# Weight conversion on a float64-fed attention and softplus kernel: fewer instructions per weight block, a planner that knows a shared port, and padded tiles

## The chip, the cores and the metric

The kernel runs on one core of a Trainium2 chip. The metric is the device time of one execution in microseconds (us). A profiled execution also has a span, from its first to its last instruction. Engines are named as in the profile: PE (TensorE matmul), PEld (its weight loads), DVE (VectorE), ACT (ScalarE), POOL (GpSimd) and SP (SyncE, which here only issues DMAs).

## The reference, cut to what matters

Attention with random features, for 8 batches, 8 heads, 576 tokens and head width 64, and then two dense layers with a softplus between them, for all 4608 tokens:

```
def phi(x):                                   # x: q or k, scaled
    proj = einsum('bhsd,md->bhsm', x, omega)  # 128 features
    h = proj - sum(x * x, -1) / 2
    return exp(h - max(h, -1)) / sqrt(m)
kv  = einsum('bhsm,bhsd->bhmd', phi(k), v);  z = sum(phi(k), axis=2)
x   = einsum('bhsm,bhmd->bhsd', phi(q), kv) / (einsum('bhsm,bhm->bhs', phi(q), z) + 1e-6)
h   = x.reshape(4608, 512) @ w_in             # 512 x 2048
g   = maximum(h, 0) + log1p(exp(-abs(h)))
out = (g @ w_out).astype(float32)             # 2048 x 512
```

`w_in` and `w_out` arrive as float64, 8 MB each. The chip computes in 32 bits, so the kernel turns each weight's two 32-bit words into a float32 first.

## The kernel before, in words

**Work and order.** Nothing loops on the chip. The kernel describes every piece of work as a `Work` with the engines that may do it and a cost on each, a due time, the works it comes after, and the buffers it takes and gives back. `in_order` then runs through them once, always starts what can start first, within a patience per engine chooses what is due first, and for work with a choice takes the engine whose clock plus cost plus a `LEAN` comes out least. `AHEAD` says how far beyond the earliest open due time it may look. The order in which it starts works is the order in which instructions are emitted, and each engine runs its instructions in that order. The due times are a table of numbers written into the calls (`due + 0.41` and so on). `with_fill` puts small idle matmuls (`fill`) into planned holes of PE in the first 70 us of the plan.

**Attention.** A quad is half a batch (4 heads); 16 of them. Each has units of 128 tokens per head pair: `plan_unit` loads q or k (`load`), squares it (`squares`, on POOL or ACT) and sums the squares (`norms`, DVE), projects with `omf` (`project`, PE), takes the row maximum (`maxima`, DVE), forms the bias in two tiny DVE instructions (`less_norms`, `bias`) and exponentiates (`exponent`, ACT). For k, `outer` accumulates k-features times v on PE. For q, `den` (DVE), `invert` (DVE), `divide` (POOL or DVE), `turn` (PE transposes) and `turned` follow, and `plan_x` makes x and splits it into two parts of reduced precision, `xh` and `xl`. The first two quads are early: they run before any dense layer can.

**Dense layers.** Tokens go in 3 blocks of 256 and 10 of 384, each in 16 steps (one per 128 columns of `w_in`), 208 steps in all. `plan_step`: `layer1` is 12 matmuls into `h`; then `magnitude`, `decay`, `log` (three ACT instructions), `plus` (DVE), `high` (DVE or ACT, writes `gh`), `low` (DVE or POOL, writes `gl`), and `layer2`, three matmuls of 512 columns for each 128 tokens.

**Weights.** There are 32 blocks of weights, 16 of `w_in` (names with `i`) and 16 of `w_out` (`o`). A step needs one of each. `plan_weights` loads a block of 512 KB as pairs of words, `low` and `high`, and converts it in 512-element instructions: `low_bits` scales the low word so that its three highest bits remain as an integer (L231 on ACT, L233 on DVE); `rebias` multiplies the high word, read as a float32, by 2^-112, which turns the float64 exponent into a float32 one (L239 ACT, L241 DVE); `high_bits` shifts it left by 3 into a tile of its own, `wt` (L245, DVE); `sign` puts the sign bit back (L249, DVE); `both` adds the low bits (L253, DVE or POOL); `high_part` rounds to the reduced precision of the matmul (L257, ACT or DVE); `low_part` keeps the rest (L260, DVE or POOL). That is seven instructions a block, 224 in all.

**Pools.** Tiles are placed one behind the other in pools. `halves`, two floats wide, is the last small tile before the loads, the weights and everything that follows.

## Time and profile before

| | |
|---|---|
| median of 3 runs | 1140.86 us (1138.83 to 1142.14) |
| the profiled execution | 1142.8 us, its span 1140.9 us |
| instructions in the profile | 19083 |
| busy, of the span | PE 1103.1 us, DVE 618.1, ACT 665.0, POOL 415.7 |
| mean granted clock of PE | 0.969 |

Busy time is a sum over the whole span, which has two very different parts: until about 175 us the weights come in, are converted, and PE has holes; after that PE has hardly any. So the profile is read by stretches of time. In the lists of groups, each row names the source line, engine, operation, what is written and read with its shape, the count, the busy time and the mean of one, and after the last bar the idle time of the engine before these instructions with what ended it. Durations of neighbouring instructions of one engine overlap a little in the records.

### The profile page before, as it was taken

What the parts mean: (1) busy time and instruction counts of PE and PEld (TensorE: products, weight loads), DVE (VectorE), ACT (ScalarE), POOL (GpSimd) and SP (SyncE); (2) the same over time, 40 slices, a digit from 0 to 9 for tenths busy, and PEclk for the clock granted to TensorE, in tenths of its full rate; (3) what the DMA queues carried; (4) which work ended last, traced back from release to release, by engine and by line L of the source; (5) the groups of instructions that cost most, each with busy time, mean ns of one, the idle gap of its engine ahead of it and who ended that gap; (6) DMA issues with size and microseconds to landing.
All of it is one profiled execution on the core that took longest, in us unless ns stands there. A gap on an engine that the chain in (4) does not pass through costs nothing.

```text
span 1140.9 us, 19083 instructions
## 1 busy us (share of the span) xinstructions
PE 1103.1 (97%) x6662; PEld 954.0 (84%) x6662; DVE 618.1 (54%) x1884; ACT 665.0 (58%) x1700; POOL 415.7 (36%) x428
## 2 busy tenths in 40 slices
PE   9887879999999999999999999999999999999998
PEld 8864768888888888888888888888888888899997
DVE  6979996777566264654364474554365356111111
ACT  4766646666666465565565565665565556455544
POOL 3638774434333233323242333333233333222222
PEclk6878889999999999999999999999999999999999
DMA  9722122331312031211222030211223020000000
GB/s 344 272 85 97 61 69 76 85 108 46 90 61 75 10 117 29 77 68 38 69 69 76 10 117 29 88 48 44 55 65 98 1 77 17 1 28 1 28 1 28
DMA packets 35088, 78.70 MB, mean 69 GB/s; under 512 B 5680, under 2 KB 12464, under 8 KB 34992
## 3 DMA queue, kind: packets, MB, share of 16 engines
q1 hardware_dynamic: 34992, 77.48, 21.2%
q8 instruction: 53, 0.87, 0.3%
q14 instruction: 43, 0.35, 0.1%
HBM read 67.99 MB, written 9.47 MB: 68 GB/s over the span
## 4 chain that ended last, share of the span: by engine, by line
PE 84%; DVE 2%; ACT 0%; issue 0%; POOL 0%; DVEq 0%
PE h L612 12%; PE acc L641 12%; PE acc L643 11%; PE acc L642 11%; PE h L614 11%; PE h L613 11%; PE kv L434 4%; PE ppq L349 3%; PE xp L568 3%; PE ppk L349 3%; PE tpq L521 2%; PE kv L429 1%; DVE smk L375 0%; DVE junk L505 0%; DVE wto L249 0%
## 5 line engine op out<-in xcount | busy, mean ns | idle before, releaser
L635 POOL TENSOR_TENSOR gl<-u,gh 128x384 fp32r<-128x384 f32 (+1 forms) x207 | 201.8, 976 | 581.8 <-ACT gh L631 507.3
L612 PE MATMUL h<-xh,wi 128*128 128x384 f32 (+1 forms) x832 | 282.7, 340 | 13.6 <-DVE u L627 11.6
L627 DVE SCALAR_TENSOR_TENSOR u<-h,u 128x384 f32<-128x384 f32 (+1 forms) x208 | 108.3, 521 | 337.7 <-ACT u L624 323.5
L614 PE MATMUL h<-xh,wi 128*128 128x384 f32 (+1 forms) x832 | 271.7, 327 | 0.0
L613 PE MATMUL h<-xl,wi 128*128 128x384 f32 (+1 forms) x832 | 271.4, 326 | 0.0
L641 PE MATMUL acc<-wo,gh 128*128 128x512 f32 x576 | 236.7, 411 | 0.3 <-ACT qq L533 0.3
L643 PE MATMUL acc<-wo,gl 128*128 128x512 f32 x576 | 228.7, 397 | 0.0
L642 PE MATMUL acc<-wo,gh 128*128 128x512 f32 x576 | 227.8, 396 | 0.0
L618 ACT ACTIVATE u<-h 128x384 f32<-128x384 f32 (+1 forms) x208 | 97.9, 471 | 218.3 <-PE h L614 212.4
L612 PEld LDWEIGHTS h<-xh,wi 128*128 128x128 f32 x832 | 158.1, 190 | 36.1 <-DVE u L627 14.9
L613 PEld LDWEIGHTS h<-xl,wi 128*128 128x128 f32 x832 | 158.5, 191 | 6.4
L614 PEld LDWEIGHTS h<-xh,wi 128*128 128x128 f32 x832 | 158.3, 190 | 0.0
L505 DVE CUSTOM_DVE_ANT_0 junk<-phq,zb 128x128 f32<-128x128 f32 x280 | 127.7, 499 | 15.7 <-ACT phq L382 14.7
L643 PEld LDWEIGHTS acc<-wo,gl 128*128 128x128 f32 x576 | 108.9, 189 | 26.0
L641 PEld LDWEIGHTS acc<-wo,gh 128*128 128x128 f32 x576 | 109.4, 190 | 24.3 <-issue 5.5
L631 ACT CAST gh<-u 128x384 fp32r<-128x384 f32 (+1 forms) x193 | 95.7, 496 | 54.7 <-PE acc L642 39.2
L642 PEld LDWEIGHTS acc<-wo,gh 128*128 128x128 f32 x576 | 109.9, 191 | 14.8
L382 ACT ACTIVATE phk<-ppk,smk 128x128 f32<-128x128 f32 x252 | 74.1, 376 | 61.5 <-DVE smk L375 59.6
L621 ACT ACTIVATE u<-u 128x384 f32<-128x384 f32 (+1 forms) x208 | 106.0, 510 | 4.3
L624 ACT ACTIVATE u<-u 128x384 f32<-128x384 f32 (+1 forms) x208 | 105.1, 505 | 4.6
L382 ACT ACTIVATE phq<-ppq,smq 128x128 f32<-128x128 f32 x252 | 73.3, 378 | 47.7 <-DVE smq L375 46.2
L514 POOL TENSOR_TENSOR phq<-phq,dnq 128x512 f32<-128x512 f32 (+1 forms) x70 | 67.2, 971 | 51.0 <-DVE dnq L510 48.8
(91 smaller groups left out, 1306.7 us busy)
## 6 DMA issues: line engine op xcount, KB each, us to landing
xk<-kx SPq DMA_DIRECT2D x28, 512.0 KB, 3.6
xq<-qx SPq DMA_DIRECT2D x28, 512.0 KB, 4.3
out<-o SPq DMA_DIRECT2D x36, 256.0 KB, 2.2
rawi<-wi SPq DMA_DIRECT2D x16, 512.0 KB, 6.1
rawo<-wo SPq DMA_DIRECT2D x16, 512.0 KB, 4.5
vk<-vv SPq DMA_DIRECT2D x28, 260.0 KB, 3.9
xk<-k SPq DMA_DIRECT2D x10, 386.0 KB, 6.8
zb<-zd SPq DMA_DIRECT2D x14, 256.0 KB, 4.4
```

The source lines that it names most:

```text
L382: nc.scalar.activation(b["ph"][:, c], b["pp"][j][:, t], AF.Exp, bias=b["sm"][:, 2, c : c + 1])
L505: nc.vector.tensor_tensor_reduce(jk[r, c], ph[r, c], q.zb[r, h], 1.0, 1e-6, ALU.mult, ALU.add, dn[r, 0, c : c + 1])
L612: nc.tensor.matmul(b["h"], wh, xh[:, cc, t], start=cc == 0, stop=False)
L613: nc.tensor.matmul(b["h"], wh, xl[:, cc, t], start=False, stop=False)
L614: nc.tensor.matmul(b["h"], wl, xh[:, cc, t], start=False, stop=cc == NCC - 1)
L621: nc.scalar.activation(b["u"], b["u"], AF.Exp, scale=-1.0)
L624: nc.scalar.activation(b["u"], b["u"], AF.Ln, bias=1.0)
L627: nc.vector.scalar_tensor_tensor(b["u"], b["h"], 0.0, b["u"], ALU.max, ALU.add)
L635: (nc.vector if e == "DVE" else nc.gpsimd).tensor_tensor(b["gl"], b["u"], b["gh"].bitcast(F32), ALU.subtract)
L641: nc.tensor.matmul(acc[tt], gh, w2[fc][:, 0], start=fc == 0, stop=False)
L642: nc.tensor.matmul(acc[tt], gh, w2[fc][:, 1], start=False, stop=False)
L643: nc.tensor.matmul(acc[tt], gl, w2[fc][:, 0], start=False, stop=fc == NFC - 1)
```

## The change

The conversion of a weight block becomes five instructions:

```
-        def rebias(e):
...
-                nc.scalar.activation(h, h, AF.Copy, scale=2.0**-112)
...
-        def high_bits():
...
-            nc.vector.tensor_scalar(box["f"], box["high"], 3, None, ALU.logical_shift_left)
-        def sign():
...
-        def both(e):
...
+        def rebias():
             h = box["high"].bitcast(F32)
+            nc.scalar.activation(h, h, AF.Prelu, scale=2.0**-112, alpha=2.0**32)
+        def joined():
+            h = box["high"]
+            nc.vector.scalar_tensor_tensor(h, h, 3, box["low"], ALU.logical_shift_left, ALU.bitwise_or)
```

The leaky ReLU (`Prelu`) multiplies negative values by a further 2^32. That raises the exponent field by 32, and the shift by 3 moves this bit to the place of the sign, while the old sign falls off. So one DVE instruction, `joined` (L253 after), shifts and ORs in the low bits, in place. For the OR, the low bits must stay in three bits: `low_bits` scales by 0.936 x 2^-29 on ACT (L241 after) or takes a minimum with 7 on DVE (L243 after). `rebias` (L249 after) is on ACT alone. `high_part` (L257) and `low_part` (L260) read the raw tile in place of `wt`, which is gone with its buffers; `NT2`, the number of those and of output tiles, goes from 3 to 2.

The planner treats DVE works that are marked `port=True`, and all POOL works, as users of one thing that only one of them can hold:

```
+    port = [0.0]
+    def ready(w, e, data):
+        return max(clock[e], data, port[0] if e == "POOL" or e == "DVE" and w.port else 0.0)
...
+        if e == "POOL" or e == "DVE" and w.port:
+            port[0] = w.end
```

Marked are the weight works on DVE, `less_norms`, `bias`, `den`, `divide`, `high` and `low`. `with_fill` also compares places in the order, not times alone, before it lends a bank. The first bank of a unit is given back after its first `exponent` as before, but that of an early query only after its second.

The planner's numbers change throughout, for instance:

```
-AHEAD = 33.61                                  +AHEAD = 43.01
-MARGIN = 0.34                                  +MARGIN = 0.00
-LEAN = {"DVE": 0.69, "POOL": -0.7, "ACT": 0.17}
+LEAN = {"DVE": 0.75, "POOL": 0.50, "ACT": 0.19}
-SPREAD = ((0, 25), (18, 63.28))                +SPREAD = ((0, 23.46), (18, 70.83))
-        l = do(("DVE", "POOL"), (dve(n), pool(n)), due - 0.48 + .2, low, ...)
+        l = do(("DVE", "POOL"), (dve(n), pool(n)), due - 1.63 + .2, low, ..., port=True)
```

`MARGIN` is what PE is planned to start after its data. Small tiles are padded, so that everything lies on multiples of 64 bytes: `halves` from 2 to 16 floats, `sm` from 3 to 4 rows of 8, `dn` from 2 to 4 rows of 4, `z` from 4 to 16, `v` to 528.

What the built programs show: POOL's rows fall from 433 to 97. Of its 207 `low` works 23 stay, of 80 `divide` 41, of 91 `squares` 14, of 26 `low_part` 8, and its 18 `both` are gone. DVE takes 185 `low` (1 before), 39 `divide` (0), 24 `low_part` (6), 12 `turned` (0); ACT takes 90 `squares` (13), 32 `rebias` (27), 32 `high_part` (26), 24 `low_bits` (26). PE's matmuls are the same but for the fills.

On DVE, in the part where steps and conversions run side by side, this stood before around the sixth step (`wti` and `wto` are the tiles that go away, `rawi` and `rawo` the loaded words):

```order
285 L245 TENSOR_SCALAR wto_1139<-rawo_671 128x512
286 L253 ISA wti_1107<-rawi_647,wti_1107 128x1024
287 L249 SCALAR_TENSOR_TENSOR wto_1139<-rawo_671,wto_1139 128x512
288 L245 TENSOR_SCALAR wti_1162<-rawi_709 128x512
289 L245 TENSOR_SCALAR wto_1167<-rawo_749 128x512
290 L249 SCALAR_TENSOR_TENSOR wti_1162<-rawi_709,wti_1162 128x512
291 L249 SCALAR_TENSOR_TENSOR wto_1167<-rawo_749,wto_1167 128x512
292 L375 SCALAR_TENSOR_TENSOR smk_0_0_1058<-smk_0_0_1058 128x4
```

and this stands there now (L635 is `low`, L627 `plus`, L260 `low_part`, L253 `joined`, L362 `maxima`):

```order
277 L635 TENSOR_TENSOR gl_4_1133<-u_4_1046,gh_4_1125 128x256
278 L253 SCALAR_TENSOR_TENSOR rawi_625<-rawi_625 128x512
279 L253 SCALAR_TENSOR_TENSOR rawo_661<-rawo_661 128x512
280 L362 TENSOR_REDUCE smk_0_0_841<-ppk_0_0_0_1114 128x4
281 L627 SCALAR_TENSOR_TENSOR u_5_1130<-h_5_1083,u_5_1130 128x256
282 L260 TENSOR_TENSOR wi_1159<-rawi_625,wi_1159 128x512
283 L253 SCALAR_TENSOR_TENSOR rawi_677<-rawi_677 128x512
284 L260 TENSOR_TENSOR wo_1168<-rawo_661,wo_1168 128x512
```

Two or three instructions for a block became one in place, and `low` and `low_part` have moved in beside it. On POOL, in the middle of the wide steps, one `low` per step stood before, with `divide` (L514) and `squares` (L333) between:

```order
197 L635 TENSOR_TENSOR gl_1_4541<-u_1_4429,gh_1_4518 128x384
198 L333 TENSOR_TENSOR xk_0_0_4544<-xk_0_0_4544 128x512
199 L635 TENSOR_TENSOR gl_2_4600<-u_2_4488,gh_2_4592 128x384
200 L635 TENSOR_TENSOR gl_3_4654<-u_3_4568,gh_3_4651 128x384
201 L514 TENSOR_TENSOR phq_0_4_4621<-phq_0_4_4621,dnq_0_4_0_4636 128x256
```

Now POOL has this there, one `low` in a dozen steps or so:

```order
58 L635 TENSOR_TENSOR gl_2_4439<-u_2_4354,gh_2_4429 128x384
59 L514 TENSOR_TENSOR phq_0_2_4433<-phq_0_2_4433,dnq_0_2_1_4493 128x512
60 L514 TENSOR_TENSOR phq_0_4_4613<-phq_0_4_4613,dnq_0_4_0_4630 128x256
61 L635 TENSOR_TENSOR gl_15_5138<-u_15_5070,gh_15_5135 128x384
62 L514 TENSOR_TENSOR phq_1_4_5268<-phq_1_4_5268,dnq_1_4_0_5289 128x256
```

and DVE, in the same wide steps, has `low` between its own work:

```order
1236 L635 TENSOR_TENSOR gl_3_6276<-u_3_6167,gh_3_6264 128x384
1237 L337 TENSOR_REDUCE smk_0_4_6279<-xk_0_4_6234 128x2
1238 L627 SCALAR_TENSOR_TENSOR u_4_6242<-h_4_6195,u_4_6242 128x384
1239 L577 TENSOR_TENSOR xl<-xp_1_0_0_6282,xh 128x256
1240 L577 TENSOR_TENSOR xl<-xp_1_0_1_6285,xh 128x256
1241 L627 SCALAR_TENSOR_TENSOR u_5_6309<-h_5_6289,u_5_6309 128x384
1242 L635 TENSOR_TENSOR gl_4_6329<-u_4_6242,gh_4_6327 128x384
```

So what POOL did behind DVE's back, DVE now does in its own queue, behind whatever stands there.

More of the change, by code (lines that the diff above doesn't have):

```diff
@@ L38 @@
 FILL = 0.3
[L39 to L41 removed]
+PATIENCE = {"PE": 0, "DVE": 0.02, "ACT": 0, "POOL": 0.00, "SP": 0.55}
+LEAN = {"DVE": 0.75, "POOL": 0.50, "ACT": 0.19}
+SPREAD = ((0, 23.46), (18, 70.83))
 VW = 512 + 4 * (D + 1)
@@ L55, with __init__ @@
 class Work:
-    def __init__(self, on, due, emit, after=(), take=(), give=(), delay=0.15, spare=0, behind=None):
-        self.on, self.due, self.emit = on, due, emit
+    def __init__(self, on, due, emit, after=(), take=(), give=(), delay=0.15, spare=0, behind=None, port=False):
+        self.on, self.due, self.emit, self.port = on, due, emit, port
         self.after = [w for w in after if w is not None]
@@ L128, in with_fill @@
     last, all_ = None, []
-    for w in out:
+    for i, w in enumerate(out):
         if w.engine == "PE":
@@ L132, in with_fill @@
             n = int((t - last - FILL) / 0.2135) if last is not None and t < until else 0
-            names = [b for b in banks if all(x1 <= last or x0 >= t for x0, x1 in held.get(b, []))] if n > 0 else []
+            names = [
+                b for b in banks if all(x1 <= last and g < i or x0 >= t and f >= i for x0, x1, f, g in held.get(b, []))
+            ] if n > 0 else []
             if names:
@@ L176, in favor_softplus_kernel @@
     nc.vector.tensor_scalar(omf, f, float(D) ** -0.25, None, ALU.mult)
-    halves = const.tile([P, 2], F32, name="halves")
+    halves = const.tile([P, 16], F32, name="halves")[:, :2]
     nc.vector.memset(halves, 0.0)
@@ L268, in plan_weights @@
         aw, dw, dw2, pw = act(DM), dve(DM), dve(DM, 2), pool(DM)
-        a = do(("ACT", "DVE"), (aw, dw2), due, low_bits, after=[l])
-        b = do(("ACT", "DVE"), (aw, dw2), due, rebias, after=[l])
-        c = do(
-            "DVE", dw2, due, high_bits, after=[b] + (in_w if last else []), take=[("wt", box, "t"), ("w", box, "w")],
+        a = do(("ACT", "DVE"), (aw, dw2), due, low_bits, after=[l], port=True)
+        b = do("ACT", aw, due, rebias, after=[l])
+        c = do("DVE", dw, due, joined, after=[a, b], port=True)
+        d = do(
+            ("ACT", "DVE"), (aw, dw), due, high_part, after=[c] + (in_w if last else []), take=[("w", box, "w")], port=True,
         )
         if not last:
-            in_w.append(c)
-        c = do("DVE", dw, due, sign, after=[c])
-        d = do(("DVE", "POOL"), (dw, pw), due, both, after=[a, c], give=[(box, "raw")])
-        e = do(("ACT", "DVE"), (aw, dw2), due, high_part, after=[d])
-        return do(("DVE", "POOL"), (dw, pw), due, low_part, after=[e], give=[(box, "t")])
+            in_w.append(d)
+        return do(("DVE", "POOL"), (dw, pw), due, low_part, after=[d], give=[(box, "raw")], port=True)
     class Quad:
@@ L385, in plan_unit @@
         ld = do(
-            "SP", dma(size), due - 5.26, load, behind=prev.get("load"),
+            "SP", dma(size), due - 5.46, load, behind=prev.get("load"),
             take=[("w" if early else "x", b, "x")], delay=DL, spare=2 if early else 0,
@@ L394, in plan_unit @@
         if not cols:
-            r = do("DVE", dve(w), due + 0.2, norms, after=[s], behind=prev.get("norms"), take=sm)
+            r = do("DVE", dve(w), due - 0.39, norms, after=[s], behind=prev.get("norms"), take=sm)
             prev["norms"] = r
@@ L536, in plan_queries @@
         d = do(
-            "DVE", 1.7 * f, due + 0.45 + .1, den, after=es + [q.zc], take=[("dn", b, "dns")],
-            give=[(q.slots, "zb")] if u == NU - 1 else [],
-        )
-        d = do("DVE", 0.09, due + 0.72, invert, after=[d])
-        v = do(("POOL", "DVE"), (1.0 * f, dve(n * M)), due + 0.45 + .2, divide, after=[d], give=[(b, "dns")])
+            "DVE", 1.7 * f, due + 1.01 + .1, den, after=es + [q.zc], take=[("dn", b, "dns")],
+            give=[(q.slots, "zb")] if u == NU - 1 else [], port=True,
+        )
+        d = do("DVE", 0.09, due + 0.48, invert, after=[d])
+        v = do(("POOL", "DVE"), (1.0 * f, dve(n * M)), due - 0.45 + .2, divide, after=[d], give=[(b, "dns")], port=True)
         t = do(
-            "PE", 0.108 * n, due - 0.16, turn, after=[v], behind=prev.get("turn"), give=[(bu, "phs" if q.b else "x")] if last else [],
+            "PE", 0.108 * n, due + 0.61, turn, after=[v], behind=prev.get("turn"), give=[(bu, "phs" if q.b else "x")] if last else [],
             take=[(any_, b, "tpb")] + ([("q", qt, "tag")] if u in (0, 2) else []),
@@ L547, in plan_queries @@
         h = do(
-            ("ACT", "DVE"), (act(n * M, PSUM), dve(n * M)), due + 1.1, turned, after=[t], give=[(b, "tpb")],
+            ("ACT", "DVE"), (act(n * M, PSUM), dve(n * M)), due + 0.97, turned, after=[t], give=[(b, "tpb")],
         )
@@ L680, in store @@
                 nc.sync.dma_start(out[t0 + tt * P : t0 + (tt + 1) * P, :], o["t"])
-            a = do("DVE", 0.34, due - 2.18, left, after=[ends[tt]], take=[("t2", o, "s")])
-            r = do("ACT", 0.27, due - 2.18, right, after=[a], give=[(box, ("acc", i, tt))])
-            do("SP", 0.75, due + 3.6, store, after=[a, r], give=[(o, "s")], delay=2.0)
+            a = do("DVE", 0.34, due + 1.48, left, after=[ends[tt]], take=[("t2", o, "s")])
+            r = do("ACT", 0.27, due - 0.39, right, after=[a], give=[(box, ("acc", i, tt))])
+            do("SP", 0.75, due + 8.51, store, after=[a, r], give=[(o, "s")], delay=2.0)
     assert NQ == 2
```

108 lines of the change are left out of this document (50 added, 58 removed).

## The prediction

> **What bounds the kernel now.** I read stretches of time first, since shares of the whole span mix two different parts. The columns are the stretch, its length, busy time (and count) of each engine, PE's granted clock, DMA share and rate.
>
> ```profile
> span 1140.9 us, 19083 instructions
> core 0: us, PE busy (x) PEld busy (x) DVE busy (x) ACT busy (x) POOL busy (x), PEclk, DMA share, GB/s
> 0.00:40.00 40.00, 37.42 (x214) 33.85 (x214) 28.38 (x105) 19.93 (x57) 18.42 (x28) 0.66 0.97 364
> 40.00:75.00 35.00, 26.44 (x186) 21.78 (x184) 29.84 (x104) 25.11 (x59) 18.17 (x14) 0.85 0.45 155
> 75.00:175.00 100.00, 78.77 (x465) 65.38 (x464) 96.04 (x190) 62.91 (x166) 68.88 (x54) 0.85 0.22 69
> 175.00:300.00 125.00, 124.52 (x930) 106.41 (x928) 86.78 (x300) 82.13 (x251) 49.62 (x62) 1.00 0.29 84
> 300.00:1100.00 800.00, 799.07 (x4698) 694.25 (x4697) 371.37 (x1177) 457.53 (x1134) 251.47 (x262) 1.00 0.16 51
> 1100.00:1141.00 41.00, 36.91 (x180) 32.35 (x178) 5.73 (x11) 17.37 (x35) 9.12 (x9) 0.98 0.05 20
> ```
>
> From 175 us on PE is full at full clock: of 925 us until 1100 it idles 1.4. The change leaves its matmuls alone, so nothing can be won there, only lost. What can be won lies before 175. The first 40 us belong to the transfers (0.97 of the DMA engines). From 75 to 175 us DVE is busy 96.0 of 100 us, while PE runs 465 matmuls in a time in which 175 to 300 runs twice as many at full clock. The list of PE's waits for 75 to 175 agrees, and so does one for 0 to 75 (line waited at, what ended it: us in total, times, longest):
>
> ```profile
> PE h L612 <- DVE u L627: 11.6, 7, 3.4
> PE xp L568 <- DVE smq L375: 4.9, 2, 4.6
> ```
>
> Why DVE is full is seen in the order of time, DVE first, then POOL (start, duration):
>
> ```profile
> 99.98 0.41 DVE L245 TENSOR_SCALAR wti<-rawi 128x512 uint32<-128x512 uint32 x1
> 105.80 0.68 DVE L249 SCALAR_TENSOR_TENSOR wto<-rawo,wto 128x512 uint32<-128x512 uint32 x1
> 106.74 1.52 DVE L245 TENSOR_SCALAR wto<-rawo 128x512 uint32<-128x512 uint32 x1
> 109.33 1.78 DVE L249 SCALAR_TENSOR_TENSOR wto<-rawo,wto 128x512 uint32<-128x512 uint32 x1
> ...
> 106.56 1.42 POOL L253 TENSOR_TENSOR wto<-wto,rawo 128x512 int32<-128x512 int32 x1 [1.57 <-DVE wto L249]
> 108.81 1.75 POOL L260 TENSOR_TENSOR wi<-wti,wi 128x512 fp32r<-128x512 f32 x1
> ```
>
> The same instruction takes 0.41 or 1.52 us, 0.68 or 1.78, and the long ones end about one short duration after the POOL instruction beside them (at 108.26 after 107.98, at 111.11 after 110.56). So DVE's time has two parts, its own work and standing behind POOL.
>
> **DVE from 75 to 175 us, term by term.** The groups of that stretch that the change touches, and one from 300 to 1100 us for the undisturbed price of the tiny bias instructions (last row):
>
> ```profile
> L249 DVE SCALAR_TENSOR_TENSOR wto<-rawo,wto 128x512 uint32<-128x512 uint32 x14 | 14.1, 1007 | 0.1
> L245 DVE TENSOR_SCALAR wto<-rawo 128x512 uint32<-128x512 uint32 x13 | 11.5, 885 | 0.0
> L249 DVE SCALAR_TENSOR_TENSOR wti<-rawi,wti 128x512 uint32<-128x512 uint32 x9 | 8.9, 984 | 0.1
> L245 DVE TENSOR_SCALAR wti<-rawi 128x512 uint32<-128x512 uint32 x9 | 7.0, 775 | 0.0
> L253 DVE CUSTOM_DVE_ANT_0 wti<-rawi,wti 128x1024 uint16<-128x1024 uint16 x5 | 5.4, 1080 | 0.0
> L253 DVE CUSTOM_DVE_ANT_0 wto<-rawo,wto 128x1024 uint16<-128x1024 uint16 x6 | 4.6, 772 | 0.0
> L375 DVE SCALAR_TENSOR_TENSOR smk<-smk 128x4 f32<-128x4 f32 x6 | 4.1, 686 | 0.1
> L370 DVE SCALAR_TENSOR_TENSOR smk<-smk 128x4 f32<-128x4 f32 x6 | 4.1, 684 | 0.0
> L260 DVE TENSOR_TENSOR wo<-wto,wo 128x512 fp32r<-128x512 f32 x3 | 3.0, 1000 | 0.0
> L260 DVE TENSOR_TENSOR wi<-wti,wi 128x512 fp32r<-128x512 f32 x2 | 2.4, 1178 | 0.0
> ...
> L375 DVE SCALAR_TENSOR_TENSOR smq<-smq 128x4 f32<-128x4 f32 x44 | 7.2, 164 | 1.5
> ```
>
> Gone are the shift, the sign, the addition and the old low parts: 14.1 + 8.9 + 11.5 + 7.0 + 5.4 + 4.6 + 3.0 + 2.4 = 56.9 us. New, counted in the built order between the first and the seventeenth step: 22 `joined` and 18 `low_part`, each two inputs of 512 as L249, undisturbed 0.68: 27.2 us; 13 `low`, at most the 0.55 us of the wide one on DVE (row below): 7.2; 2 `divide` of 512, at 0.68: 1.4. `joined` reads both words at a step of two and `low_bits` gains a minimum; before has both steps and pairs of operations in other rows at the same price, so I take no extra; doubling `joined` is the upper end, 15 us. The 12 bias instructions fall from 8.2 to 12 x 0.164 = 2.0. Sum: 96.0 - 56.9 + 27.2 + 7.2 + 1.4 - 6.2 = 68.7 us.
>
> What is left of the standing: the ten rows lost 56.9 + 8.2 us less their undisturbed 23 x 0.68 + 22 x 0.41 + 11 x 0.68 (the addition taken as the sign) + 5 x 0.68 + 2.0 = 37.5, so 27.6 us beside 68.9 us of POOL, 0.40 for each. POOL keeps some 10 us there (a few `low_part`, `low`, `divide`, `squares`), so 4 us, and none where the planner's port keeps them apart. The page SBUF — State Buffer of the Trainium skill, section Who interferes with whom, speaks against this: the pair of ports is an exclusive lock, an instruction with two inputs in SBUF contends for it, and the later one blocks fully, whatever its size. By it the whole 10 us could fall on DVE, 78.7 in place of 72.7; the row's share is what this order of work showed, and I keep it.
>
> **ACT and PE in that stretch.** ACT's prices, and what the squares cost that it takes over:
>
> ```profile
> L239 ACT ACTIVATE rawo<-rawo 128x512 f32<-128x512 f32 x9 | 6.1, 674 | 0.0
> L257 ACT CAST wo<-wto 128x512 fp32r<-128x512 f32 x11 | 6.8, 617 | 7.9 <-DVE wto L253 5.2 <-POOL wto L253 2.6
> L331 ACT ACTIVATE xk<-xk 128x512 f32<-128x512 f32 x1 | 0.6, 614 | 0.0
> ```
>
> By the order it has there 16 `rebias` (14 before), 22 `high_part` (19), 9 `low_bits` (10), 4 squares (2): +0.67 x 1 + 3 x 0.62 + 2 x 0.61 = 3.8, so 66.7 us. A Prelu I price as the scaling it replaces, 0.67. PE needs 465 x 124.52/930 = 62.3 us at full clock. So DVE falls from 96 to about 70, and ACT (67) and PE (62) stand right beside it. Before, the stretch took 1.04 of its busiest engine. Three nearly full engines that wait for each other in turn will not do that; I take 77 us, 1.1 times DVE's 70. Ends: 69, nothing lost between them, and 92, where the chains of one step after the other cost 22. **Gain 23 us, 8 to 31.**
>
> **The stretch to 75 us.** Until 40 us transfers bound it, and the change moves no byte: nothing. From 40 to 75 DVE is busy 29.8 of 35 us. By the order, before the first step DVE now has 10 `joined` and 6 `low_part`, 5 `divide` that POOL did, and one `den` group less; eight squares go from POOL to ACT, which has room (25.1 of 35). The conversions shrink and the divisions eat half of that: 4 us, 0 to 10.
>
> **After 175 us: nothing won, a little lost.** `low` and `divide` go to DVE:
>
> ```profile
> L635 POOL TENSOR_TENSOR gl<-u,gh 128x384 fp32r<-128x384 f32 x150 | 153.4, 1022 | 478.3 <-ACT gh L631 426.3 <-DVE gh L631 11.9 <-DVE smq L370 11.0
> L635 DVE TENSOR_TENSOR gl<-u,gh 128x384 fp32r<-128x384 f32 x1 | 0.5, 549 | 0.0
> ```
>
> That is some 150 x 0.55 + 30 x 0.68 = 103 us on a DVE that is busy 371 of 800: it stays under 60%, and each `low` itself is 0.47 us shorter. The squares add 30 x 0.61 = 18 us to ACT's 457. I take nothing. Two output tiles in place of three do cost at the end, where each of the last three copies has gone to a tile of its own:
>
> ```profile
> 1136.95 0.42 DVE L674 COPY o<-acc 128x256 f32<-128x256 f32 x1 [0.28 <-PE acc L643]
> 1136.41 1.73 SPq L680 DMA_DIRECT2D out<-o  x3
> out<-o SPq DMA_DIRECT2D x36, 256.0 KB, 2.2
> ```
>
> The third must now wait until the first store, issued at 1136.41, has landed 2.2 us later: 1138.6 in place of 1136.95, 1.6 us. In earlier blocks PE runs up to three steps ahead, which covers it; without that cover it is 9 x 1.6 = 15 us. Padding I take at nothing. Matmuls of 128x256 and of 128x512 in order of time:
>
> ```profile
> 172.81 0.28 PE L613 MATMUL h<-xl,wi 128*128 128x256 f32 x1
> 172.93 0.28 PE L614 MATMUL h<-xh,wi 128*128 128x256 f32 x1
> ...
> 173.27 0.39 PE L642 MATMUL acc<-wo,gh 128*128 128x512 f32 x1
> 174.90 0.40 PE L643 MATMUL acc<-wo,gl 128*128 128x512 f32 x1
> ```
>
> The first streams `xl`, which lies ahead of the 8-byte `halves`, on a multiple of 64; it starts the next 0.12 us later, 0.47 ns a column. The second streams `wo`, behind it and off the multiple; seven starts in 1.63 us are 0.233 each, 0.45 ns a column. So no loss is seen that padding could take away.
>
> **Sum.** The profiled execution took 1142.8 us: - 23 - 4 + 1.6 gives 1117.4. It stands 1.9 us over the median of the runs, 1140.86, so 1115 for the median.
>
> **The rivals.**
>
> A, less comes of it: DVE's room is real, but each step's chain through PE, ACT, DVE, ACT, DVE and PE, and the bias pairs between, set the pace. For it: from 75 to 175 us ACT waited for DVE and PE too, and it is busy only 63 of 100. Against: nearly all PE waits name DVE. Stretch 92 us or more, nothing before 75: 1140.9 - 8 + 1.6 = 1134.
>
> B, more comes of it: the stretch runs at DVE's floor and the early part saves its 10 us: 1140.9 - 31 - 10 + 1.6 = 1101.
>
> C, slower, by one mechanism: `low` on DVE comes late to PE in the steady part. POOL was idle 478 us before its 150 `low`s, so each began when `gh` was there; on DVE it stands in the queue behind a maximum or a group of `den`, and PE is no longer planned with a margin of 0.34 us. Behind one instruction of 0.68 us it is 0.21 late (0.68 less the 0.47 won), with the margin 0.55. On half of the 192 steps after the first block that is 53 us: 1115 + 53 = 1168. It decides from 26 us, 0.14 us for each of 192 steps. Against it: the order lets `layer1` run up to three steps ahead of `layer2`, in 182 of 208 steps, as in 175 before.
>
> D, the Prelu brings table loads. The trace has one:
>
> ```profile
> L146 ACT ACT_TABLE_LOAD x1 | 1.3, 1283 | 0.7 <-PEq L831 0.7
> ```
>
> The Prelus stand in 19 groups between exponentials and logarithms; two loads for each are 38 x 1.283 = 49 us on ACT, some 30 of them from 75 to 175 us: 67 + 30 = 97, DVE's place of before. That gives the old time, and with 19 us more in the early part about 1155. Against it: the built order has one load, as before, where Abs, Exp, Ln and squares lie side by side too. ScalarE: Activation LUTs of the Trainium skill, section Table sets: the hidden batching unit, says that functions come in sets and each change of set is a load; its section What ACT_TABLE_LOAD costs adds a drain, 2.66 us together, which would make it 101 us. No run here shows which set holds Prelu.
>
> **Chances.** My forecast 0.62, A 0.14, B 0.14, C 0.06, D 0.04. The range takes in A and B and the ends of the stretch terms, 1097 to 1137, and leaves out C, D and the outer part of B. About 0.3%, 3.4 us, is what a measurement of this kernel can tell from no change, so faster means under 1137.4: forecast, B and most of A, 0.88; the same 0.04; slower 0.08.
>
> **What would show it.** If right: from the first to the seventeenth `magnitude` it takes about 77 us; DVE's L253, after, near 0.68 us in the mean and L374 near 0.16; POOL under 100 us in all; PE's loss after that unchanged, about 1 us in 800; ACT's L249 at 0.67 with one table load; the last copy some 2 us after PE's last matmul. It is wrong if `joined` is far over 0.68, if PE waits in the steady part for `gl` or DVE, or if the first `magnitude` is no earlier than 75 us and the steps after it still come every 6 us.

## The result, and the profile after

The kernel before took 1141.16 us in the median of its runs here (1138.83 to 1142.14), the changed one 1093.55 us (1090.80 to 1098.19): 0.959 of the time, 95% interval 0.9547 to 0.9632. The prediction had the direction and the place, and half of the size: 47.6 us were won where 26 were forecast, and the time lies below the range. In the ratios and medians below, a run more than 1.5% above the fastest of its kernel on the same occasion is left out.

The page of the changed kernel, span and busy times:

```profile
span 1094.3 us, 18824 instructions
...
PE 1083.9 (99%) x6670; PEld 944.3 (86%) x6670; DVE 630.0 (58%) x2083; ACT 691.4 (63%) x1773; POOL 77.6 (7%) x92
```

Its stretches, cut at its first step and its seventeenth, with the columns as in the prediction:

```profile
0.00:40.00 40.00, 37.58 (x204) 33.76 (x204) 22.11 (x103) 23.63 (x69) 4.86 (x14) 0.62 0.95 346
40.00:71.70 31.70, 30.99 (x222) 27.33 (x223) 23.29 (x106) 26.26 (x62) 6.48 (x5) 0.83 0.59 209
71.70:131.20 59.50, 58.25 (x421) 50.49 (x420) 55.78 (x161) 59.50 (x162) 8.99 (x9) 1.00 0.30 88
131.20:300.00 168.80, 168.80 (x1216) 145.44 (x1216) 110.25 (x400) 115.13 (x340) 19.21 (x23) 1.00 0.27 78
300.00:1055.00 755.00, 755.00 (x4455) 657.85 (x4454) 408.98 (x1300) 450.89 (x1115) 38.10 (x41) 1.00 0.18 52
1055.00:1095.00 40.00, 33.27 (x163) 29.41 (x162) 9.64 (x18) 16.02 (x32) 0.00 (x0) 0.96 0.06 20
```

The third of these rows is the one to look at. In the 59.50 us from the first to the seventeenth step ACT is busy for all 59.50, PE for 58.25 and DVE for 55.78, with POOL at 9. The same cut of before has DVE alone at its limit:

```profile
75.40:174.60 99.20, 77.97 (x461) 65.00 (x462) 95.80 (x189) 62.52 (x165) 68.48 (x54) 0.85 0.23 70
```

The cuts are the first and the seventeenth `magnitude` (start, duration), of before and then of the changed kernel:

```profile
75.42 0.39 ACT L618 ACTIVATE u<-h 128x256 f32<-128x256 f32 x1 [2.91 <-PE h L614]
174.63 0.37 ACT L618 ACTIVATE u<-h 128x256 f32<-128x256 f32 x1
```

```profile
71.69 0.42 ACT L618 ACTIVATE u<-h 128x256 f32<-128x256 f32 x1
131.19 0.40 ACT L618 ACTIVATE u<-h 128x256 f32<-128x256 f32 x1
```

So the span, which fell from 1140.9 to 1094.3, splits into three terms:

| | before | after | difference | forecast |
|---|---|---|---|---|
| to the first step | 75.4 | 71.7 | -3.7 | -4 |
| first to seventeenth step | 99.2 | 59.5 | -39.7 | -23 |
| seventeenth step to the end | 966.3 | 963.1 | -3.2 | +1.6 |

DVE's groups between the two cuts, those that the prediction priced:

```profile
L253 DVE SCALAR_TENSOR_TENSOR rawo<-rawo 128x512 uint32<-128x512 uint32 x13 | 8.8, 684 | 0.3 <-ACT rawo L249 0.2
L260 DVE TENSOR_TENSOR wo<-rawo,wo 128x512 fp32r<-128x512 f32 x11 | 7.5, 684 | 1.3 <-ACT wo L257 1.2
...
L253 DVE SCALAR_TENSOR_TENSOR rawi<-rawi 128x512 uint32<-128x512 uint32 x9 | 6.1, 683 | 0.0
L635 DVE TENSOR_TENSOR gl<-u,gh 128x256 fp32r<-128x256 f32 x13 | 5.4, 418 | 0.3 <-ACT gh L631 0.3
L260 DVE TENSOR_TENSOR wi<-rawi,wi 128x512 fp32r<-128x512 f32 x7 | 4.8, 684 | 0.0
...
L369 DVE SCALAR_TENSOR_TENSOR smk<-smk 128x4 f32<-128x4 f32 x6 | 2.0, 339 | 0.1
...
L374 DVE SCALAR_TENSOR_TENSOR smk<-smk 128x4 f32<-128x4 f32 x6 | 0.9, 154 | 0.0
```

`joined` and `low_part` take 0.684 us each, all 40 of them between 0.675 and 0.694: none of them stands behind POOL any more. A trace of it is left in the bias row L369, 339 ns in the mean where L374, the instruction after it, takes 154.

PE waits once in that stretch, for 1.2 us, and the program loads one table of functions:

```profile
PE h L612 <- DVE smq L369: 1.2, 1, 1.2
```

```profile
0.73 1.28 ACT L156 ACT_TABLE_LOAD   x1 [0.73 <-PEq L830]
```

At the end the third copy waits for a store to land, as forecast:

```profile
1086.95 0.42 DVE L674 COPY o<-acc 128x256 f32<-128x256 f32 x1 [1.84 <-PE acc L643]
1087.63 0.42 DVE L674 COPY o<-acc 128x256 f32<-128x256 f32 x1 [0.26 <-PE acc L643]
1089.95 0.42 DVE L674 COPY o<-acc 128x256 f32<-128x256 f32 x1 [1.90 <-DMA out<-o]
```

### The profile page after: what moved, and what is told of

It is laid out like the page before. It is cut to its first block, busy times and chain, and to the rows that moved or that the text cites. A ratio compares the mean times of both kernels' runs of the same rounds, so it can differ in the third digit from the quotient of the medians.

```text
span 1094.3 us, 18824 instructions
## 1 busy us (share of the span) xinstructions
PE 1083.9 (99%) x6670; PEld 944.3 (86%) x6670; DVE 630.0 (58%) x2083; ACT 691.4 (63%) x1773; POOL 77.6 (7%) x92
## 4 chain that ended last, share of the span: by engine, by line
PE 95%; ACT 3%; DVE 1%; DMA 1%; issue 0%; SPq 0%; ACTq 0%; DVEq 0%
PE h L612 14%; PE acc L641 12%; PE h L613 12%; PE h L614 12%; PE acc L642 12%; PE acc L643 12%; PE kv L434 6%; PE ppk L348 4%; PE ppq L348 4%; PE xp L568 3%; PE tpq L521 3%; PE kv L429 1%; ACT xq L381 1%; PE fill L747 0%; DMA xk<-k 0%; PE ppq L357 0%
## 5 line engine op out<-in xcount | busy, mean ns | idle before, releaser
L627 DVE SCALAR_TENSOR_TENSOR u<-h,u 128x384 f32<-128x384 f32 (+1 forms) x208 | 108.8, 523 | 226.4 <-ACT u L624 225.8
L641 PE MATMUL acc<-wo,gh 128*128 128x512 f32 x576 | 231.6, 402 | 0.0
L642 PE MATMUL acc<-wo,gh 128*128 128x512 f32 x576 | 225.8, 392 | 0.1
L643 PE MATMUL acc<-wo,gl 128*128 128x512 f32 x576 | 224.8, 390 | 0.0
L612 PEld LDWEIGHTS h<-xh,wi 128*128 128x128 f32 x832 | 156.1, 188 | 21.1 <-issue 4.5
L613 PEld LDWEIGHTS h<-xl,wi 128*128 128x128 f32 x832 | 156.3, 188 | 4.9
L614 PEld LDWEIGHTS h<-xh,wi 128*128 128x128 f32 x832 | 156.4, 188 | 0.0
L635 DVE TENSOR_TENSOR gl<-u,gh 128x384 fp32r<-128x384 f32 (+1 forms) x185 | 98.1, 531 | 76.2 <-ACT gh L631 74.6
L641 PEld LDWEIGHTS acc<-wo,gh 128*128 128x128 f32 x576 | 108.1, 188 | 18.2 <-issue 2.4
L642 PEld LDWEIGHTS acc<-wo,gh 128*128 128x128 f32 x576 | 108.3, 188 | 13.5 <-DVE wo L260 0.4
L505 DVE CUSTOM_DVE_ANT_0 junk<-phq,zb 128x128 f32<-128x128 f32 x280 | 100.8, 399 | 17.5 <-ACT phq L381 16.8
L362 DVE TENSOR_REDUCE smk<-ppk 128x4 f32<-128x512 f32 (+2 forms) x104 | 53.9, 520 | 19.4 <-PE ppk L348 19.2
```

What stands on the lines that cost most here:

```text
L505: nc.vector.tensor_tensor_reduce(jk[r, c], ph[r, c], q.zb[r, h], 1.0, 1e-6, ALU.mult, ALU.add, dn[r, 0, c : c + 1])
L612: nc.tensor.matmul(b["h"], wh, xh[:, cc, t], start=cc == 0, stop=False)
L613: nc.tensor.matmul(b["h"], wh, xl[:, cc, t], start=False, stop=False)
L614: nc.tensor.matmul(b["h"], wl, xh[:, cc, t], start=False, stop=cc == NCC - 1)
L627: nc.vector.scalar_tensor_tensor(b["u"], b["h"], 0.0, b["u"], ALU.max, ALU.add)
L641: nc.tensor.matmul(acc[tt], gh, w2[fc][:, 0], start=fc == 0, stop=False)
```

## The experiments

In the table, "steps" is the time from the first to the seventeenth `magnitude`, "rest" from there to the end of the span, both of the one profiled execution; the time is the median of the runs, with the ratio to the kernel before on the same chip and its 95% interval.

| kernel | time, us | ratio | first step | steps | rest |
|---|---|---|---|---|---|
| changed (the result) | 1093.55 | 0.959 (0.9547 to 0.9632) | 71.7 | 59.5 | 963.1 |
| changed again | 1082.61 | 0.950 (0.9474 to 0.9525) | 56.3 | 61.6 | 962.9 |
| before + new conversion | 1111.52 | 0.9749 (0.9721 to 0.9776) | 66.6 | 77.4 | 966.8 |
| changed, old conversion | 1119.83 | 0.9804 (0.9752 to 0.9856) | 74.9 | 90.3 | 955.8 |
| changed, planner without the port | 1094.74 | 0.9606 (0.9545 to 0.9666) | 56.9 | 64.2 | 968.6 |
| changed, `low_part` on DVE twice | 1106.73 | 0.9702 (0.966 to 0.9744) | 62.4 | 74.0 | 962.4 |
| changed, `high_part` on ACT twice | 1108.70 | 0.9715 (0.9679 to 0.975) | 68.0 | 76.1 | 961.6 |
| before + padding | 1140.01 | 1.0009 (0.999 to 1.0027) | 70.6 | 98.1 | 966.7 |
| changed, no paddings | 1087.17 | 0.9552 (0.9507 to 0.9597) | 56.2 | 62.1 | 968.3 |
| changed + third tile | 1082.31 | 0.9517 (0.9475 to 0.9559) | 55.8 | 59.6 | 961.3 |
| the same, no paddings | 1087.03 | 0.9552 (0.9513 to 0.9591) | 57.3 | 62.0 | 966.6 |

One thing has to be known to read the times: single runs of the changed kernel and its relatives differ by the clock that PE was granted in the first 70 us (section on the control), so single runs are compared at equal mean clock, and the columns of the profile count for more than the medians.

Four runs are left out: 1095.23 us with the third tile (mean clock 0.980), 1100.84 (0.979) and 5622.38 us (1.000) without the paddings, and 1103.48 us (0.996) of the kernel with all `low` on POOL further down. The low clock goes with the first two. No profile was taken of the other two, and what held them up is not known.

### The conversion alone, and the schedule alone

The new conversion put into the kernel before, with that kernel's numbers, paddings and planner (this edit and the next in words, not line by line):

```
 before:  plan_weights: rebias (ACT or DVE), high_bits, sign, both, ...
+         plan_weights: rebias = Prelu (ACT), joined (DVE), ...     # nothing marked for the port
-         room["wt"] = ...
```

> The kernel before with the new conversion of a weight tile alone (Prelu, one joined instruction: five instead of seven); the schedule doesn't know the port, its numbers are those of before, the paddings too. POOL keeps 31 low parts, 95 squares, 80 divisions and 207 low parts of g. Theory S (DVE's time behind POOL is the larger part of the gain): DVE stays nearly full in the steps 1 to 17, which take 80 to 90 us, and the time is 1115 to 1128. Rival N (the two instructions fewer are the larger part): the steps 1 to 17 take 62 to 72 us and the time is 1098 to 1110.

and the old one put into the changed kernel:

```
 changed: numbers, port rule, paddings as changed
-         rebias = Prelu (ACT), joined (DVE)
+         rebias (ACT or DVE), high_bits, sign, both (all DVE/POOL works marked port=True)
+         room["wt"] = ...                          # with NT2 = 2, one buffer fewer than before
```

> The changed kernel with the old conversion of a weight tile (seven instructions, its DVE and POOL ones marked for the port); numbers of the schedule, rule of the port and paddings are the new ones. POOL keeps 5 'both', 4 low parts, 6 squares, 40 divisions and 21 low parts of g. Theory A (the two halves of the gain add up: the shorter conversion alone took 21.8 of the 39.7 us off the steps 1 to 17): those steps take 78 to 84 us, the rest from the 17th 963 us, and the time is 1104 to 1118 by the head's clock. Rival (with seven instructions all on DVE, the freed POOL is worth nothing, since DVE has to take over what POOL did): 90 us or more, 1118 to 1130.

The stretch between the two cuts, first of the one and then of the other:

```profile
66.60:144.00 77.40, 66.75 (x450) 55.94 (x451) 63.71 (x149) 57.92 (x156) 50.89 (x43) 0.96 0.30 93
```

```profile
74.90:165.20 90.30, 77.36 (x519) 64.51 (x518) 85.17 (x246) 65.88 (x180) 10.45 (x10) 0.92 0.25 76
```

The conversion alone takes 21.8 us off the steps, the schedule alone 8.9 (POOL falls from 68 to 10 us, and DVE, which takes over its work, from 96 of 99 to 85 of 90), both together 39.7 or, in the control below, 37.6: 7 to 9 more than the sum. The schedule alone had to do with three buffers for converted words in place of four; what that cost it was not tried. The first kernel lies between theory S and rival N, nearer to S in its steps and to N in its time; the shorter conversion is the larger part of the gain in either order, 21.8 of the 39.7 us when it comes first and 30.8 when it comes last. For the second the rival was right, 90 us. We read it so: DVE needs room before POOL's work can be moved to it, and the conversion makes that room. (The rest of the second kernel is short, 955.8, because its longer stretch has taken in more of PE's work: 78 fewer rows of matmuls come after it.)

### The port in the planner

```
-        return max(clock[e], data, port[0] if e == "POOL" or e == "DVE" and w.port else 0.0)
+        return max(clock[e], data)
```

> The changed kernel whose schedule no longer knows the port (POOL and DVE are planned as if apart); the numbers and all else as changed. POOL takes 9 low parts, 20 squares, 55 divisions and 54 low parts of g, where the changed kernel gives it fewer. Theory T (the rule itself keeps DVE from standing behind POOL): the steps 1 to 17 take 65 to 70 us instead of 59.5 to 61.6, and the time at an equal mean clock is 4 to 9 us above the control's (1080 at 0.999, 1091 at 0.985). Rival U (the new numbers, which make POOL dear, do it alone): 59 to 63 us and within 2 us of the control at an equal clock.

```profile
56.90:121.10 64.20, 60.70 (x426) 50.70 (x425) 61.28 (x161) 59.77 (x158) 18.74 (x19) 1.00 0.32 99
```

DVE's busy time rises from 56.5 (the control, below) to 61.3 us with 161 instructions in place of 164, beside a POOL that is busy for 18.7 in place of 9.0 us. The steps take 64.2 us, 2.6 to 4.7 more, a little under what theory T said, and the rest 5.6 more. At a mean clock of 0.995 the run took 1091.5 us, where the control, on another chip, took 1082.6 at 0.996 and 1084.3 at 0.994. So the rule is worth some 8 us of the 47, as theory T had it in sum. Its mechanism, DVE behind POOL, is seen in the steps, in 2.6 to 4.7 of those 8 us. Of the 5.6 after them PE's visible waits are 2.9 us; the remainder is not explained.

### Which engine paces the steps now

```
-            (nc.vector if e == "DVE" else nc.gpsimd).tensor_tensor(w[fc][:, 1], ...)
+            for _ in range(2 if e == "DVE" else 1):
+                (nc.vector if e == "DVE" else nc.gpsimd).tensor_tensor(w[fc][:, 1], ...)
```

> The changed kernel with every low part of a weight on DVE computed twice (0.68 us each, 17 of them or 11.6 us in the steps 1 to 17; same result). Theory V (DVE paces these steps as it did before, its 4 us of idle time being all the slack): the steps take 67 to 71 us and the time grows by 7 to 10 us. Rival W (ACT and PE pace them; DVE's instructions there are short of a bound): 59 to 64 us, under 3 us.

```
-            (nc.vector.tensor_copy if e == "DVE" else nc.scalar.copy)(w[fc][:, 0], ...)
+            for _ in range(2):
+                (nc.vector.tensor_copy if e == "DVE" else nc.scalar.copy)(w[fc][:, 0], ...)
```

> The changed kernel with every high part of a weight on ACT copied twice (0.70 us each; about 20 in the steps 1 to 17, some 13.6 us, and some 6 us before; same result). Theory W (ACT, busy for 59.00 of these 59 us, paces them now): 71 to 76 us, the time 14 to 20 us longer. Rival V (ACT is only full of work that could have waited): under 5 us in the steps, the time under 6 us longer.

```profile
62.40:136.40 74.00, 65.36 (x435) 53.74 (x434) 70.77 (x184) 61.65 (x162) 10.24 (x9) 0.98 0.24 73
```

```profile
68.00:144.10 76.10, 65.06 (x424) 54.29 (x422) 55.63 (x158) 74.17 (x183) 8.87 (x9) 0.96 0.23 71
```

The groups show 17 extra `low_part` in the first kernel, 12.5 us, and 22 extra `high_part` in the second, 13.7 us. Against the steps of the changed kernel, 59.5 and 61.6 in two profiles, they cost 12.4 to 14.5 and 14.5 to 16.6 us: each in full, though the two are on different engines. V and W, written as rivals, are both right that their own engine paces the steps and wrong about the other, and both costs came out at or above the upper end (V said 67 to 71 us, W 71 to 76). DVE's 4 us of idle time was no slack. We read the reason from the order of work: a block passes from ACT to DVE, ACT and DVE, and what is late on one is late on the other. The planner was not told of the doubled instructions, so this holds for an order that stays as it is; an order planned around them was not tried.

### The control, and the clock in the first 70 us

The changed kernel, unaltered, run again later:

> The changed kernel, unaltered, as a control beside the others. Theory H (the clock granted to TensorE in the first 75 us differs from run to run, and it alone spreads the times of the changed kernel): single runs with a mean clock of 0.995 or more take 1085 to 1089 us, runs at 0.986 and below 1089 to 1098 us, in one order; the median lies anywhere between 1087 and 1097. In the profile the first step starts near 56 us where the clock stays at 1.00, near 72 us where it is at 0.50 for 40 us. Rival P (the multiples of 64 bytes cost or bring several us): the median lies 5 us or more away from the 1087.17 of the kernel without paddings at equal clocks.

```profile
0.00:40.00 40.00, 37.35 (x298) 32.76 (x300) 33.02 (x148) 33.99 (x94) 7.82 (x15) 1.00 0.96 361
40.00:56.30 16.30, 15.02 (x120) 12.42 (x116) 13.08 (x56) 15.50 (x37) 4.97 (x4) 0.95 1.00 377
56.30:117.90 61.60, 61.53 (x431) 53.92 (x431) 56.53 (x164) 59.75 (x161) 8.98 (x9) 0.96 0.28 83
```

Against the first three rows of the changed kernel above: the granted clock of the first 40 us is 1.00 in place of 0.62, PE does 298 rows of matmuls there in place of 204, and the first step starts at 56.3 in place of 71.7 us. From the seventeenth step on the two profiles agree to 0.2 us. In between the control's steps are 2.1 us longer, at a clock of 0.96 in place of 1.00, and there PE is the engine without a gap (61.53 of 61.60 us). The single runs of both occasions lie in one order of clock and time: 0.999 gives 1080.1, 0.996 1082.6, 0.994 1084.3, 0.985 1090.8 and 1091.0, 0.980 1096.1, 0.977 1098.2 us. Theory H holds in its order and in the place of the first step, not in its numbers: the runs at 0.996 and above took 1080 to 1083 us, not 1085 to 1089. Those numbers came from the kernel without paddings below, whose clock was also at 1.00 in the first 40 us and which took 1085.5 and 1085.9 us at 0.999. That is 5 us more than the control at the same clock, so the rival P is right as well: clock and paddings both count.

What brings the clock down? Two kernels tried to hold it:

```
-        fill("at.0", 8, idle)                    # the first kernel
+        fill("at.0", 16, idle)
...
+            if force and t >= force[0]:          # the second, in with_fill; force = [13.0, 21.0, 29.0]
+                n = max(n, 16)
```

> The changed kernel with 16 instead of 8 idle matmuls ahead of the first feature matmul (1.9 us more of PE work before 5 us; no effect on the output), and with the third output tile of the last block in a free tile of x. Theory H1 (the clock falls at 8 to 12 us because PE waits 0.76 + 0.27 + 0.23 us for the first chunks of k): no such waits, clock 1.00 to 20 us and beyond, first step near 56 to 60 us, median 1086 to 1089 with mean clocks of 0.995. Rival H2 (the clock falls at some point of the narrow matmuls between 10 and 45 us whatever comes before): the same spread as the control, median 1088 to 1096, and the drop later than 12 us in the profile. Tail, under both: the last DVE copy no longer waits 1.90 us for a store, the span ends 4.0 to 4.3 us after PE's last matmul instead of 6.0, which is worth 1.7 to 2.0 us.

> The changed kernel with the same third output tile, and with three bursts of 16 idle matmuls (2.05 us each at full clock, 3.8 us at half clock; no effect on the output) put between the narrow matmuls of the first 45 us. Theory H2 (a stretch of full-width matmuls of some 3 us gives the clock back, as the 16 fills at 45.9 us did in the profile of the changed kernel): the clock is back at 1.00 within 4 us of each burst, the first step starts at 58 to 64 us in every run, the median is 1086 to 1090 and the spread within 4 us. Rival H3 (the clock comes back by time, not by work): 0.50 for some 40 us in some runs all the same, and the bursts cost up to 10 us there: 1093 to 1105.

With 16 fills no wait for a chunk of k is left in the profile (one of 0.72 us for ACT is), and still four of six runs had mean clocks of 0.985 to 0.987 and took 1089.5 to 1089.9 us, and two had 0.998 and 1.000 and took 1081.2 and 1080.0. That speaks for H2: the clock falls without those waits too, in the profile itself at 27 us, for 3.4 us. (The median, 1089.53, says nothing but that.) With the bursts, the clock came back within the first of them. Its wide matmuls, and the clock around it:

```profile
18.05 6.09 PE L752 MATMUL fill<-ident 128*128 128x128 f32 x32
```

```profile
20.00:22.00 2.00, 2.00 (x12) 2.00 (x11) 0.00 (x0) 0.00 (x0) 0.00 (x0) 0.50 0.94 287
22.00:24.00 2.00, 2.00 (x15) 1.94 (x14) 0.00 (x0) 0.00 (x0) 1.37 (x3) 0.79 0.85 273
24.00:26.00 2.00, 1.94 (x24) 1.69 (x23) 1.06 (x4) 0.00 (x0) 0.53 (x2) 1.00 0.80 285
```

All its runs have mean clocks of 0.993 to 1.000, but the control's five on the same chip have 0.994 to 0.999, so the means alone show nothing. And the time was 1088.3 to 1096.3 us (median 1093.27, 0.9589 of before, 0.9563 to 0.9616): for 6 us DVE and ACT stand still behind the burst, and the first step starts at 72.2 us. The clock part of H2 held in this profile; its time, first step and spread did not, and H3's time was nearer. One reason is in the rows. An idle matmul of the program is two rows of the profile (8 at the start are 16 rows), so 16 of them are 32 rows, 3.84 us where the clock was full, while the expectation took its 2.05 us from a run of 16 rows. What decides in which run the clock falls stays open.

### The paddings

```
-    halves = const.tile([P, 16], F32, name="halves")[:, :2]      # and v, sm, z, dn likewise
+    halves = const.tile([P, 2], F32, name="halves")
```

> The changed kernel with its five paddings undone; the order of instructions is the same. Theory P (padding): a 128x512 matmul that streams w_out off a multiple of 64 bytes costs about 5 ns more (232 against 227 from start to start in the traces of before and after), so 1728 of them give back 9 us: about 1102, the matmuls into acc at 0.260 us in the mean as before (0.2547 after). Rival Q (quiet POOL): the faster matmuls come from an almost idle POOL, not from addresses: time stays at 1093, mean stays 0.255.

The reverse, `halves` padded in the kernel before, which puts its `w`, `u`, `gh` and `gl` on multiples of 64:

> The kernel before with `halves` alone padded from 2 to 16 floats, which puts all weights and gh, gl, u on multiples of 64; same order. P: 9 us faster than before, about 1132, matmuls into acc at 0.255 us. Q: 1141, 0.260.

Neither came out as a theory had it: the first was not slower in its median, and the second changed nothing. The profiles say more than the medians, since the first had the clock at 1.00: its rest is 968.3 us, 5.2 over that of the changed kernel. Two half-way kernels moved one half off the multiple by 32 bytes, first the weights, then the tiles of `u` and `g`:

```
+    ff.tile([P, 8], F32, name="shift", tag="shift", bufs=1)       # both: 32 bytes ahead of u and g
-    halves = const.tile([P, 16], F32, name="halves")[:, :2]       # weights off: 32 bytes less ahead of all
+    halves = const.tile([P, 2], F32, name="halves")
```

> The changed kernel with the weights 32 bytes off a multiple of 64 (halves 2 floats wide again) but gh, gl and u put back on it by a spare 32-byte tile. P, streamed operand: matmuls into acc 0.260 as in before, since w_out is streamed there; P, stationary operand: 0.255, as in after. Q: 0.255.

> The changed kernel with the weights on multiples of 64 and gh, gl, u 32 bytes off by a spare 32-byte tile. P, streamed operand: matmuls into acc stay at 0.255; P, stationary operand: 0.260. Q: 0.255.

Their rests are 968.4 and 968.2 (one run each, 1102.8 and 1091.59 us), and from one matmul into `acc` to the next it is 232 and 233 ns where the changed kernel has 227. It takes both halves, which neither version of theory P had. To settle it on one chip, with and without the paddings, and with a third output tile for the last block in both (`o` from a free buffer of `x`):

```
+    room["last"] = room["t2"] + room["x"]
...
-            a = do("DVE", 0.34, due + 1.48, left, after=[ends[tt]], take=[("t2", o, "s")])
+            a = do("DVE", ..., take=[("last" if i == len(sizes) - 1 else "t2", o, "s")])
```

> The changed kernel with the third output tile of the last block in a free tile of x, and nothing else. The last copy should start 0.7 us after the one before instead of 2.3 us, and the time at an equal mean clock lie 1.5 us below the changed kernel's (1078.5 at 0.999, 1089.5 at 0.985). Rival (the store on the queue, not the copy, ends the span): no gain.

> The same as the kernel with the third output tile, but without the five paddings, on the same chip. Theory P (aligned operands of the matmuls into acc are worth 5 ns each, 1728 of them in the steps after the first block and before): at an equal mean clock 4 to 6 us slower, 232 ns in place of 227, 966 to 967 us from the 17th step to the end in place of 961. Rival Q (the difference seen so far was that of two chips): within 1.5 us at an equal clock, the same ns.

Rests of 961.3 and 966.6 us; single runs of 1078.5 and 1083.9 at a mean clock of 0.999, 1082.3 and 1086.4 at 0.996, 1090.9 and 1096.8 at 0.984. Theory P, 4 to 6 us. From one matmul into `acc` to the next it is 227 ns with and 232 without (median of the starts after 250 us). The 9 us that theory P first said are too many: behind the seventeenth step there are 1640 such matmuls, not 1728, and their mean differs by 3.4 ns, not 5, which is 5.5 us. The third tile does its part too; the last copies are now

```profile
1070.97 0.42 DVE L674 COPY o<-acc 128x256 f32<-128x256 f32 x1 [1.84 <-PE acc L643]
1071.65 0.42 DVE L674 COPY o<-acc 128x256 f32<-128x256 f32 x1 [0.26 <-PE acc L643]
1072.33 0.42 DVE L674 COPY o<-acc 128x256 f32<-128x256 f32 x1 [0.26 <-PE acc L643]
```

and the rest is 1.6 us shorter than the control's. This is the version to keep: at equal clocks it lies 0 to 1.6 us below the changed kernel, and its fastest run, 1078.47 us, is the fastest seen.

Why did padding bring nothing in the kernel before? The first guess was POOL, which computed `gl` there:

```
-        l = do(("DVE", "POOL"), (dve(n), pool(n)), due - 1.63 + .2, low, ...)
+        l = do("POOL", pool(n), due - 1.63 + .2, lambda: low("POOL"), ...)
```

> The changed kernel with all 208 low parts of g on POOL (the kernel before had most there); paddings and all else as changed. Theory R (a busy POOL takes away what the paddings bring): 232 ns from one matmul into acc to the next, 967 to 969 us from the 17th step to the end. Rival L (another part of the layout keeps the kernel before at 232 ns): 227 ns, 962 to 964 us, plus whatever PE then waits for gl, which the waits would name. In the steps 1 to 17, under both: 13 such instructions of some 1 us on POOL beside DVE, 0 to 5 us more.

POOL was busy 151 of 700 us in the steady part, and matmuls into `acc` kept their 227 ns and the rest its length, 961.9: theory R fell. (The steps took 67.0 us in place of 59.5 to 61.6, more than was expected, and the time was 1087.07 us, 0.9572 of before, 0.9523 to 0.9621.) What was left is where `g` lies. In the built programs the changed kernel has `wo` and `gh` both at 192 modulo 512 bytes, the padded kernel before `wo` at 192 and `gh` at 320. So the changed kernel's `u` and `g` were moved by 128 bytes:

```
-            q.z = at.tile([P, 16], F32, ...)[:, :4]
+            q.z = at.tile([P, 32], F32, ...)[:, :4]
```

> The changed kernel with its tiles of u and g 128 bytes further on (still on multiples of 64, now where the padded kernel before had them modulo 512). Theory G (more than the multiple of 64 counts in the place of g): 232 ns from one matmul into acc to the next and 968 us from the 17th step to the end. Rival (the place of g within 512 bytes is nothing): 227 ns and 963 us.

The view by tile gives count, and least, median and longest duration in ns; first the changed kernel, then this one:

```profile
L643 PE MATMUL acc<-wo,gl x342: 387/389/398, 401.5 to 998.6; 128*128 128x512 f32 x171
```

```profile
L643 PE MATMUL acc<-wo,gl x341: 388/393/404, 402.8 to 999.7; 128*128 128x512 f32 x171
```

232 ns again from start to start, and a rest of 968.0 (1086.5 and 1096.2 us at mean clocks of 0.998 and 0.985): theory G. It is not the multiple of 64 that counts, or not that alone.

## Why the prediction was wrong

**The step that failed** is the term of the stretch from 75 to 175 us, "77 us, 1.1 times DVE's 70", with its lower end of 69. Its mechanism was right: DVE was the bound, its shorter conversion and the end of its standing behind POOL made the gain, and ACT, PE and DVE then stood side by side. Both factors were too large. The busiest engine had 59.5 us of work, not 70, and the stretch took 1.00 of it, not 1.1.

**DVE's sum, 68.7 us and 4 of standing, measured 55.8.** The rows that were priced came out right: `joined` and `low_part` 27.2 us in the sum, 8.8 + 6.1 + 7.5 + 4.8 = 27.2 in the groups. Summed over its rows DVE fell by 41.6 us, and the sum had 27.3. The missing 14 lie in rows that it didn't list or priced otherwise:

- 13 `low` are 256 wide and take 0.418 us, not the 0.55 of the wide one: 1.8 us.
- The bias instructions on `smk` are 16, not 12; the four narrow ones were in rows of another shape: 1.7.
- The changed conversion also takes two `rebias` of 1.49 us and four `high_part` off DVE, less two more `low_bits`: 3.8.
- The sum kept all side work of 100 us in a stretch that ends at the seventeenth step. The units are due by time, so the shorter stretch holds fewer of them: a group of four `den` and the maxima and biases of queries went past its end, or got shorter, some 7 us.

The last point also explains a part of PE (58.3 in place of 62.3; of its 40 rows fewer 12 are idle fills) and a part of ACT (59.5 in place of 66.7; the eight exponentials of that group). For ACT there is one more: its durations grew while its busy time fell,

```profile
L257 ACT CAST wo<-rawo 128x512 fp32r<-128x512 f32 x13 | 8.9, 692 | 0.0
```

692 ns where the same copy showed 617 before. Its rows between the cuts add up to 85.0 us in 59.5. Instructions that follow each other without a gap overlap in the records, so adding instructions at their row's mean to the busy time of an engine with gaps gives too much.

**What stands behind POOL.** The prediction kept 4 us, and named the rule of the Trainium skill (SBUF — State Buffer, section Who interferes with whom) by which it could be 10. Visible is less: the six L369 of four columns exceed their twins by 6 x 0.185 us and two narrow ones by some 0.8, 2 us beside 9 us of POOL. All rows of DVE in the stretch can be set against a short duration of the same instruction (the 20th percentile over the traces of this case); it is an estimate. By it DVE stood some 35 us before, beside 68 of POOL, 19 beside 51 with the conversion alone, 9 beside 19 with the port out of the planner, and 2 beside 9 in the changed kernel. That is a quarter to a half; no run here shows DVE losing the whole of POOL's time. It also says that of the 40 us by which DVE fell some 32 were standing, and 8 its own work.

**The factor 1.1.** PE's waits before named DVE's `u` in 11.6 us; after, one wait of 1.2 us is left. Three nearly full engines did not lose anything to each other. The two doublings show that this is no sign of slack. Rival A, a pace set by chains, fell; B, the floor, had the right idea and a floor that was 10 us too high.

**After the seventeenth step** the forecast was +1.6 and the profile has -3.2. The tail came as worked out (the span ends 2.0 us later after PE's last matmul than before; the third tile takes 1.6 of it back). The paddings, taken at nothing, brought 5.2. The step that failed is the reading that the matmul that streams `wo` "off the multiple" loses nothing: it set 0.45 ns a column against 0.47 of another shape, where only the same shape in another place could have told.

**What held.** `joined` at 0.684 us, L374 at 0.154, POOL at 77.6 us, one table load (rival D fell), PE full from 131 to 1055 us with 185 `low` on DVE (rival C fell), and the last copy 2 us after PE's last matmul. That the first 75 us came out as forecast (-3.7 for -4) is luck: in the control, at full clock, the first step starts at 56.3 us, 19 us before the old one. No case spoke of the clock in the head, which spreads single runs of the changed kernel from 1080.1 to 1098.2 us: the control was 11 us faster than the result.

## What to carry to other kernels

When the bound of a stretch is cut, sum the work that is tied to the stretch (steps, blocks) and leave out what is due by time, since a shorter stretch holds less of it; and list every row of the engine, the small and odd shapes too, for a third of DVE's fall lay there. Work moved off a shared port pays only if the engine that takes it has room: conversion and schedule brought 21.8 and 8.9 us apart and 39.7 together. When a kernel's runs spread, compare the rows of its profiles by stretch and the runs at equal clock before a median is believed.

## What the hardware showed that was not expected

The clock of PE was granted at 0.50 from some 10 to 50 us in the one profile, with PE busy without a gap from 16 to 48 us, and at 1.00 in the other, with the same program (the changed kernel, then the control):

```profile
24.00:32.00 8.00, 8.00 (x45) 7.25 (x44) 4.91 (x22) 5.45 (x15) 0.06 (x1) 0.50 1.01 367
```

```profile
24.00:32.00 8.00, 7.75 (x72) 6.81 (x72) 7.74 (x40) 8.00 (x22) 1.72 (x3) 1.00 1.01 389
```

The Trainium skill's page TensorE: Matmul & The Clock Gate, Part 1, says that half rate ends after one busy window of some 3.4 us. The trace does not agree, if a busy window is one in which the profile shows PE busy: the 45 rows of matmuls in these 8 us, of 2 to 130 columns or with 64 rows of weights, did not end it. It came back at some 50.6 us, 4.7 us into a run of 128 by 128 matmuls (16 rows of fills and then `zp`), and in the kernel with bursts 4.8 us into one. That the size of the matmuls decides is a guess from these places and was not tried by itself. It is not all of it: two fills and eight 128 by 128 matmuls into `zp`, one behind the other, left the clock at 0.50 at 36 us in the changed kernel, and at the end of the same ten rows it came back at 30 us in the kernel with 16 fills.

A matmul of 512 columns took 227 ns from start to start when the operand that it streams (`wo`) and the one that it holds (`gh` or `gl`) both lay at 192 modulo 512 bytes, and 231 to 234 ns when either was 32 bytes off or when the held one lay 128 bytes further. Nothing here shows which residues are good ones, nor why.
